# RG-LRU and multiplicative feed-forward on one core: the order of the jobs and the engines of some of them set anew

## The chip, the core and the metric

The kernel runs on one core of a Trainium2 chip, in one launch. The metric is the device time of that launch in microseconds (us): the median of three runs before the change is 511.52 us (511.37, 511.52 and 512.6).

## The reference

A gated linear recurrence over time (RG-LRU) is followed by a multiplicative feed-forward network. Four sequences of 5824 steps and 256 channels come in as `x`, with a recurrence gate `r_gate` and an input gate `i_gate` of the same shape.

```python
log_a = 8.0 * sigmoid(r_gate) * log(sigmoid(a_param))
a_t   = exp(log_a)
x_g   = sqrt(max(1 - a_t * a_t, 1e-6)) * sigmoid(i_gate) * x
h     = a_t[:, t] * h + x_g[:, t]          # for each t, h = 0 at t = 0
y[:, t] = h
out   = (((y @ w1) * (y @ w2)) @ w3) @ w_out   # 256 -> 1024, 1024 -> 1024 -> 256
```

The kernel folds `w3 @ w_out` once into one matrix of 1024 x 256, so a token costs two products of 256 x 1024 and one of 1024 x 256.

## The kernel before

The 23296 tokens (batch and time in one row) are cut into 47 chunks: two of 256 tokens (chunks 0 and 1, whose gates are computed together as chunk 0), 44 of 512 and a last one of 256. Each chunk goes through a chain of small jobs. A job is written as a letter with the chunk's number, then the number of the half, the quarter or the bank:

- `r`, `i`, `x` load a chunk's gate and input rows (SyncE's DMA queue, SP in the profile), `o` stores output rows.
- `R`, `I` are the two tanh on ScalarE (ACT); a sigmoid is 0.5 (1 + tanh).
- `V` turns the recurrence gate so that channels lie on partitions: by TensorE (PE, line 200) for the chunks in `TURN_R`, by a transposing DMA for all others.
- `d` is the decay a_t on ACT (line 223), one job for each half of the channels, and `s` its square (lines 231 and 233).
- `q` is the square root on ACT (line 238), in place in the tile `nrm`.
- `p` (1 + tanh) runs on GpSimd (POOL); `t` multiplies it by x, into the tile `u_t` (lines 189 and 192). `U` turns u as `V` does the gate.
- `g` combines root and u on VectorE (DVE, lines 248 and 251). `h` is the scan over time, DVE's alone (line 270). `y` casts it to bfloat16 (lines 280 and 282).
- `a` and `b` are the two up-projections on PE (line 299). `a` fills one bank of 512 columns, which `c` copies to SBUF (tile `sa`, lines 320 on DVE and 322 on ACT). `b` fills two banks, which `m` multiplies by `sa` on DVE, into `g_t` (line 337).
- `D` is the down-projection on PE (line 357), `e` copies its output out of PSUM (tile `ot`).
- `Lw`, `Cw` load and cast weights; `Ft`, `Fc`, `Fm`, `Fe` fold w3 and w_out in eight pieces (line 425 transposes, line 436 multiplies into `pw`); `W` is a pair of warm matmuls whose result is not used (line 287).

So `a4.2.1` is the first up-projection of chunk 4, third quarter, second half of it, and `m4.2` the product of that quarter.

There are 2449 jobs. One string, `ORDER`, lists them all, and the loop below it calls each in turn, so an engine executes its jobs in the order in which the string names them. Nothing reorders them on the engine: a job that waits holds up what stands behind it on that engine. Sets of tuples say which engine does a job that several can do: `DV_COPY` for `c`, `DV_EVAC` for `e`, `DV_SQUARE` and `AC_SQUARE` for `s` (POOL otherwise), `DV_HALF` for `t`, `DV_CAST` and `AC_CAST` for `y` (POOL otherwise), `FOLD_ACT` for `Fc` and `Fe` (DVE otherwise).

Buffers are rings (`RINGS`), taken in the order of the string. PSUM has four banks in the ring `po`, which `a`, `V`, `U`, `Ft`, `Fm` and `D` share, and two pairs of banks in the ring `pb` for `b` and `W`. A matmul that takes a bank waits until the one four back (two back for `b`) has been read.

Of the kernel before, what the change touches and what calls it, by code (L numbers as in the profile page):

```python
# [23 lines left out]
def kernel(  # L24
# [150 lines left out]
    def times(c, half):  # L175
# [15 lines left out]
        else:  # L191
            (nc.vector if (c, half) in DV_HALF else nc.gpsimd).tensor_mul(out=u, in0=t, in1=xt)  # L192

# [31 lines left out]
    def square(c, cb):  # L225
# [6 lines left out]
        else:  # L232
            (nc.vector if (c, cb) in DV_SQUARE else nc.gpsimd).tensor_mul(out=n, in0=a, in1=a)  # L233

# [37 lines left out]
    def cast(c, cb=None):  # L272
# [8 lines left out]
        else:  # L281
            (nc.vector if key in DV_CAST else nc.gpsimd).tensor_copy(out=y, in_=h)  # L282

# [190 lines left out]
    def last(c):  # L474
# [26 lines left out]
        Lw3.4 x3 Lw3.3 Lw3.6 Lw3.7 r7 m0.2 h2.0 h2.1 R3 a1.2.1 a1.2.0 a0.3.0 c1.3.0 c0.3.0 Fm2 b0.3 b1.2 V3 R4 V4
        c1.2.0 d3.1 d4.0 d3.0 d4.1 m0.3 b1.3 y2 Fe2 m1.2 m1.3 a2.0.0 a2.0.1 b2.0 a2.1.0 c2.0.1 c2.0.0 c2.1.0 m2.0
        Cw3.0 s3.1 Cw3.5 Cw3.1 b2.1 a2.2.1 Ft0 a2.1.1 Fc0 Ft1 c2.1.1 Fc1 s4.0 I3 s4.1 c2.2.1 a2.2.0 Ft5 Fm0 p3 Cw3.4
        c2.2.0 Fc5 m2.1 s3.0 q3 Cw3.3 Fe0 b2.3 Fm1 q4 Fe1 Ft4 t3.0 t3.1 U3 Fc4 g3 h3.0 h3.1 Cw3.6 Cw3.7 b2.2 Fm5 Fm4
        a2.3.1 Ft7 R7 Fe5 Fe4 Fc7 r5 i4 r6 x4 i5 i6 i7 c2.3.1 a2.3.0 Ft3 R5 I4 c2.3.0 Fc3 Ft6 Fm7 y3 a3.2.1 Fc6 Fm3
        m2.3 R6 Fe7 c3.2.1 V7 m2.2 Fe3 d7.1 a3.2.0 c3.2.0 d7.0 b3.2 Fm6 a3.3.1 a3.0.0 a3.3.0 m3.2 Fe6 c3.0.0 I5 c3.3.1
        s7.0 I6 V5 r8 i8 V6 r9 x5 b3.3 d5.1 a3.0.1 d5.0 c3.0.1 c3.3.0 m3.3 p4 t4.0 t4.1 p5 s7.1 U4 a3.1.1 c3.1.1 s5.0
        I7 I8 D0.1 D0.0 b3.0 b3.1 a3.1.0 g4 h4.0 h4.1 s5.1 R8 R9 d6.0 d6.1 p6 y4 p8 t5.0 t5.1 D0.3 D0.2 m3.0 e0.0
        c3.1.0 a4.1.1 b4.1 a4.3.1 D2.0 D2.1 s6.1 q7 e2.0 q5 s6.0 x6 p7 t6.0 t6.1 c4.1.1 e0.1 m3.1 c4.3.1 x7 x8 o0.0
        i10 r11 V9 o2.0 a4.0.1 a4.1.0 c4.0.1 c4.1.0 m4.1 a4.2.0 b4.3 a4.3.0 U5 g5 h5.0 h5.1 c4.2.0 c4.3.0 q6 D2.3 D2.2  # L510
        e2.1 r12 r10 V8 o2.1 o0.1 i9 i11 x10 a4.0.0 U6 D3.0 a4.2.1 D3.1 b4.0 c4.0.0 I10 c4.2.1 e3.0 d9.1 d9.0 m4.3 g6
        y5 t8.1 t7.1 t7.0 m4.0 a5.1.0 b4.2 a5.1.1 a5.0.1 a5.0.0 b5.0 c5.1.1 c5.1.0 c5.0.0 m4.2 h6.1 U7 a5.3.1 c5.0.1
        s9.1 R10 c5.3.1 R11 d8.1 I9 m5.0 g7 h6.0 b5.1 D3.3 b5.3 D3.2 a5.2.1 a5.3.0 e3.1 R12 d8.0 m5.1 c5.2.1 c5.3.0
        h7.1 D4.2 a5.2.0 D4.3 e4.1 m5.3 i13 V10 o3.0 x9 p10 t8.0 y6 p9 s8.0 s9.0 h7.0 b6.0 a6.0.0 a6.0.1 y7 c5.2.0 I11
        I13 a6.2.1 a6.2.0 b5.2 s8.1 c6.0.0 c6.0.1 c6.2.0 D4.1 a6.1.0 D4.0 d10.1 c6.2.1 d10.0 e4.0 q9 a6.1.1 m6.0 m5.2
        U8 o3.1 i12 r15 V11 r13 t9.1 t9.0 U9 V12 a6.3.0 b6.1 c6.1.1 c6.1.0 m6.1 a6.3.1 b6.2 a7.1.1 b6.3 a7.1.0 m6.2
        t10.0 s10.1 p11 t10.1 o4.0 o4.1 r16 i14 i16 c6.3.0 q8 c6.3.1 m6.3 g8 h8.0 h8.1 g9 c7.1.1 c7.1.0 a7.3.0 a7.0.0
        a7.0.1 b7.1 c7.3.0 R15 c7.0.0 c7.0.1 D6.0 D6.1 a7.3.1 D5.0 D6.2 b7.3 D6.3 D5.1 d11.1 c7.3.1 e6.0 s11.1 I12
        d11.0 d12.1 m7.1 h9.1 y8 a7.2.1 a8.2.0 b7.0 e6.1 m7.3 p12 s11.0 p13 s10.0 e5.0 a8.2.1 a7.2.0 c7.2.1 I16 c8.2.1
        s12.1 m7.0 c8.2.0 a8.0.1 b7.2 c8.0.1 c7.2.0 a8.0.0 c8.0.0 m7.2 D5.2 D5.3 b8.0 a8.1.1 d12.0 R13 q10 q11 c8.1.1  # L520
        I14 x11 o6.0 t11.0 t11.1 U10 r14 x12 o6.1 x13 V13 b8.2 D7.1 D7.0 h9.0 m8.0 g10 e5.1 y9 t12.1 V15 U11 o5.0 o5.1
        m8.2 b8.1 a8.1.0 c8.1.0 a9.1.0 a9.0.1 h10.0 h10.1 m8.1 e7.0 R16 c9.1.0 c9.0.1 d13.1 a9.0.0 b9.0 c9.0.0 D7.2
        a8.3.1 a9.1.1 D7.3 c9.1.1 R14 d15.0 e7.1 c8.3.1 y10 p16 a8.3.0 b9.1 d13.0 o7.0 x15 x14 i15 V14 o7.1 r17 t13.0
        p14 s13.1 t12.0 t13.1 m9.0 m9.1 a10.0.0 b8.3 d15.1 c8.3.0 c10.0.0 s12.0 s15.1 a9.2.1 a10.3.1 a10.0.1 b10.0
        a9.2.0 c9.2.1 m8.3 g11 c10.3.1 c10.0.1 m10.0 c9.2.0 d14.0 b9.2 D8.1 a10.3.0 a9.3.1 D8.0 h11.0 c10.3.0 e8.0
        d14.1 I15 D8.2 D8.3 e8.1 V16 d16.0 s13.0 a9.3.0 b10.3 d16.1 c9.3.1 h11.1 m9.2 U12 U13 r19 o8.0 r20 i17 x16 i19
        a10.2.0 a10.2.1 b9.3 a10.1.1 c10.2.1 c10.2.0 R17 m10.3 c9.3.0 m9.3 b10.2 c10.1.1 s14.0 y11 p15 t14.0 s16.1
        t15.1 t15.0 s16.0 t14.1 a10.1.0 a11.0.1 c10.1.0 m10.2 c11.0.1 a11.1.0 a11.3.0 b10.1 a11.0.0 a11.1.1 c11.1.0
        m10.1 q12 s14.1 c11.3.0 c11.0.0 q13 a11.2.0 b11.0 c11.1.1 g12 m11.0 b11.1 D10.3 a11.3.1 D10.2 s15.0 q14
        c11.2.0 c11.3.1 e10.1 a11.2.1 b11.3 D10.0 q15 D10.1 e10.0 c11.2.1 q16 D9.1 h12.0 h12.1 g13 y12 m11.1 h13.1  # L530
        h13.0 a12.0.1 b11.2 D9.2 a12.0.0 D9.0 D9.3 c12.0.1 R19 c12.0.0 U15 x17 U14 o8.1 o10.1 V17 d17.0 I17 r18 r23
        y13 V19 m11.3 m11.2 e9.0 e9.1 b12.0 m12.0 a13.0.0 a12.2.0 c12.2.0 b12.1 a12.1.0 t16.0 t16.1 U16 o10.0 o9.0 g14
        h14.0 h14.1 a12.1.1 c13.0.0 R18 c12.1.0 g15 a13.0.1 d17.1 V18 a12.2.1 b12.2 d19.0 D11.0 R20 c12.1.1 c12.2.1
        c13.0.1 r21 p17 y14 s19.0 D11.1 D11.2 a12.3.0 D11.3 m12.1 b13.0 e11.0 d19.1 e11.1 m12.2 d18.0 a12.3.1 a14.0.0
        s18.0 m13.0 c12.3.0 I19 c12.3.1 a13.1.0 b12.3 i20 V20 x19 b14.0 a14.0.1 c14.0.0 h15.0 d18.1 a13.1.1 m12.3
        c14.0.1 a13.2.0 s17.0 t17.0 c13.1.0 c13.2.0 m14.0 c13.1.1 b13.1 a14.1.0 m13.1 R21 a14.1.1 a13.2.1 i18 c14.1.0
        I20 c13.2.1 c14.1.1 r22 o9.1 V21 t17.1 o11.0 h15.1 a13.3.0 b14.1 g16 m14.1 i21 o11.1 c13.3.0 D12.0 D12.1 h16.0
        I18 a13.3.1 a14.2.1 b13.2 a14.2.0 m13.2 c13.3.1 e12.0 o12.0 d20.0 d20.1 p19 R22 c14.2.0 D12.2 b13.3 D12.3
        c14.2.1 y15 s18.1 b14.2 a15.0.0 a15.0.1 e12.1 m13.3 c15.0.0 c15.0.1 s19.1 m14.2 a15.1.0 a14.3.0 a15.1.1 h16.1
        p20 s20.0 c15.1.0 c15.1.1 b15.0 c14.3.0 m15.0 b15.1 a14.3.1 a15.2.0 x20 a15.2.1 x18 D13.0 r25 U17 R23 x21  # L540
# [124 lines left out]
```

## Time and profile before

| what | us |
|---|---|
| median of three runs | 511.52 |
| lowest and highest | 511.37, 512.6 |
| span of the profiled execution | 509.1 |
| median less that span | 2.4 |

The profiled execution is one run of the program on the chip, and its span runs from its first to its last instruction; of its time only this span is shown. A row of the timeline has the start, the duration, the engine, the line, the operation, output and inputs with their shapes, how many instructions are merged in it, and, in brackets, how long the engine had been idle and what released it. A group's row has the busy time of all its instructions, the mean duration of one in ns, and the idle time before them. PEld is the loading of weights into the array, which goes on beside the matmuls.

### The profile page before, as it was taken

Reading aid. Unit: us, or ns where it says so; the run is one execution under the profiler, and the core shown is the slowest. Engines: PE = TensorE matmul, PEld = TensorE weight load, DVE = VectorE, ACT = ScalarE, POOL = GpSimd, SP = SyncE. Lnnn points to the kernel's source line nnn. Section 1 sums busy time; section 2 is a strip of 40 time slices with the busy share of each in tenths; the row PEclk is TensorE's granted clock in tenths of the full one; section 3 lists DMA queues with packets and bytes.
Section 4 is the critical chain, followed back from the end, with each engine's and each line's share of the span. In section 5 each row is a group of like instructions: output and inputs, shape, how many; then the busy total and the mean of one; then the engine's idle time right before and its main releaser. Section 6 shows DMA issues by size and latency. Waiting matters only on the chain.

```text
span 509.1 us, 8891 instructions
## 1 busy us (share of the span) xinstructions
PE 501.7 (99%) x3225; PEld 308.3 (61%) x3225; DVE 431.8 (85%) x417; ACT 461.5 (91%) x708; POOL 318.0 (62%) x269
## 2 busy tenths in 40 slices
...
GB/s 317 410 411 345 335 316 282 305 286 259 310 220 298 279 285 247 211 302 196 247 305 327 254 286 148 252 243 227 210 246 164 235 298 161 85 166 62 65 51 104
DMA packets 178048, 124.06 MB, mean 244 GB/s; under 512 B 87378, under 2 KB 174036, under 8 KB 178004
## 3 DMA queue, kind: packets, MB, share of 16 engines
...
## 4 chain that ended last, share of the span: by engine, by line
PE 92%; ACT 3%; DMA 2%; POOL 1%; DVE 1%; issue 1%; SPq 1%; ACTq 0%; DVEq 0%
PE po L357 30%; PE pb L299 29%; PE pa L299 29%; DMA wf<-in_moe_w_dram 2%; PE pw L436 1%; ACT sa L322 1%; PE ptr L200 1%; PE ptw L425 1%; POOL u_t L192 0%; DVE h_t L270 0%; SPq L151 0%; ACT ot L322 0%; SPq L407 0%; ACT L168 0%; ACT L238 0%
## 5 line engine op out<-in xcount | busy, mean ns | idle before, releaser
L337 DVE TENSOR_TENSOR g_t<-sa,pb 128x1024 bf16<-128x1024 bf16 (+1 forms) x188 | 218.7, 1180 | 58.9 <-PE pb L299 27.6
L299 PEld LDWEIGHTS <-w_sb 128*128 128x128 bf16 x1504 | 146.4, 98 | 144.1 <-issue 1.4
L322 ACT CAST sa<-pa 128x512 bf16<-128x512 f32 (+1 forms) x332 | 179.8, 591 | 27.1 <-PE pa L299 18.9
L299 PE MATMUL pa<-y_t,w_sb 128*128 128x512 bf16 (+1 forms) x752 | 190.2, 372 | 0.2 <-ACT sa L322 0.2
L299 PE MATMUL pb<-y_t,w_sb 128*128 128x512 bf16 (+1 forms) x752 | 184.9, 372 | 0.2 <-ACT w_sb L414 0.2
L357 PE MATMUL po<-wp_sb,g_t 128*128 128x256 bf16 (+1 forms) x1464 | 177.6, 272 | 0.0
L357 PEld LDWEIGHTS <-g_t 128*128 128x128 bf16 x1464 | 142.5, 98 | 39.5 <-issue 0.3
L282 POOL CAST y_t<-h_t 128x1024 bf16<-128x1024 f32 (+2 forms) x47 | 53.8, 1145 | 140.2 <-DVE h_t L270 136.1
L192 POOL TENSOR_TENSOR u_t<-i_t,x_t 128x512 bf16<-128x512 f32 (+1 forms) x90 | 123.3, 1387 | 3.8 <-DMA ut<-u_t 1.8
L270 DVE TENSOR_TENSOR_SCAN h_t<-a_t,h_t,nrm 128x512 f32<-128x512 f32 (+1 forms) x92 | 121.1, 1343 | 1.6
L233 POOL TENSOR_TENSOR nrm<-a_t 128x512 f32<-128x512 f32 x70 | 78.4, 1137 | 7.0 <-ACT a_t L223 4.0
L223 ACT ACTIVATE a_t<-rt,la 128x512 f32<-128x512 bf16 (+1 forms) x82 | 66.1, 823 | 0.0
L322 ACT COPY ot<-po 128x512 f32<-128x512 f32 x84 | 49.1, 589 | 13.2 <-PE po L357 12.9
L173 POOL TENSOR_SCALAR i_t<-i_t 128x1024 f32<-128x1024 f32 (+1 forms) x45 | 55.4, 1233 | 8.3 <-ACT i_t L168 8.3
L251 DVE SCALAR_TENSOR_TENSOR nrm<-nrm,ut 128x1024 f32<-128x1024 f32 (+1 forms) x39 | 53.2, 1365 | 5.2 <-ACT nrm L238 5.2
L168 ACT ACTIVATE i_t<-i_t 128x1024 f32<-128x1024 f32 (+1 forms) x46 | 48.5, 1063 | 0.3 <-DMA i_t<-in_i_gate_dram 0.2
L238 ACT ACTIVATE nrm<-nrm 128x1024 f32<-128x1024 f32 (+1 forms) x47 | 48.4, 1040 | 0.2
L162 ACT ACTIVATE th_r<-r_t 128x1024 bf16<-128x1024 f32 (+1 forms) x41 | 43.5, 1064 | 0.0
L320 DVE CAST sa<-pa 128x512 bf16<-128x512 f32 x36 | 23.5, 684 | 1.4 <-PE pa L299 0.8
L238 ACT ACT_TABLE_LOAD x17 | 21.8, 1283 | 0.4
L287 PE MATMUL warm<-ident 128*128 128x512 bf16 x32 | 10.7, 473 | 1.6 <-DVE ident L441 1.6
L231 ACT ACTIVATE nrm<-a_t 128x512 f32<-128x512 f32 x18 | 11.4, 645 | 0.0
...
## 6 DMA issues: line engine op xcount, KB each, us to landing
...
wf<-in_moe_w_out_dram SPq DMA_DIRECT2D x2, 512.0 KB, 10.2
rt<-th_r SPq DMA_TRANSPOSE x41, 4.7
ut<-u_t SPq DMA_TRANSPOSE x39, 4.4
```

The lines of the kernel that those rows point to most:

```text
L173: (nc.vector if c in DV_PLUS else nc.gpsimd).tensor_scalar(t, t, 1.0, 1.0, op0=ALU.add, op1=ALU.mult)
L192: (nc.vector if (c, half) in DV_HALF else nc.gpsimd).tensor_mul(out=u, in0=t, in1=xt)
L223: nc.scalar.activation(out=a, in_=pr, func=AF.Exp, scale=la4[:, cb:cb + 1], bias=la4[:, cb:cb + 1])
L233: (nc.vector if (c, cb) in DV_SQUARE else nc.gpsimd).tensor_mul(out=n, in0=a, in1=a)
L238: nc.scalar.activation(out=n, in_=n, func=AF.Sqrt, scale=-1.0, bias=1.0)
L251: nc.vector.scalar_tensor_tensor(out=n, in0=n, scalar=1e-3, in1=T["pu", c][:, :, cols], op0=ALU.max, op1=ALU.mult)
L270: nc.vector.tensor_tensor_scan(h[:, cb, :], a[:, cb, :], n[:, cb, :], init, ALU.mult, ALU.add)
L282: (nc.vector if key in DV_CAST else nc.gpsimd).tensor_copy(out=y, in_=h)
L299: nc.tensor.matmul(out=dst, lhsT=w_sb[:, cb, m * P:(m + 1) * P], rhs=T["y", gates_of(c)][:, cb, span(c, mp)], start=(cb == 0), stop=(cb == ...
L322: nc.scalar.copy(out=dst, in_=src_ps)
L337: nc.vector.tensor_mul(out=T["g", z][:, 2 * mp:2 * mp + 2, span(c, mp)], in0=T["sa", c, mp][:, :, :w], in1=T["pb", c, mp][:, :, :w])
L357: nc.tensor.matmul(out=po, lhsT=T["g", c][:, k, j * P:(j + 1) * P], rhs=wp_sb[:, k, cols], start=(k == 0), stop=(k == KD - 1), skip_group_ ...
```

## The change

The string `ORDER` is new up to the jobs of chunk 24, and the same, job for job, behind that. The sets of engines are new up to chunk 28. No job is added, dropped or computed in another way; tiles, rings and DMA sizes are the same. A part of the diff, the sets:

```diff
-    DV_HALF = set()
-    DV_SQUARE = {(0, 0), (0, 1), (5, 1), (9, 0)}
...
-    DV_CAST = {(1, 1)}
-    AC_CAST = {(1, 0)}
+    DV_HALF = {(5, 0), (17, 0)}
+    DV_SQUARE = {(0, 0), (0, 1), (3, 1), (13, 0), (18, 1), (19, 1), (21, 0), (23, 1), (24, 1), (28, 0)}
...
+    DV_CAST = {24, (0, 1), (1, 1)}
+    AC_CAST = {14}
...
-    DV_EVAC = {(0, 0), (0, 1), (4, 1), (5, 1), (6, 1), (9, 0), (9, 1)}
-    FOLD_ACT = {('e', 0), ('e', 4), ('e', 5), ('e', 7)}
+    DV_EVAC = {(0, 0), (0, 1), (4, 0), (5, 1), (6, 1), (9, 0), (9, 1), (12, 1), (13, 0), (20, 0), (22, 1)}
+    FOLD_ACT = {('e', 0), ('e', 3), ('e', 4), ('e', 5), ('e', 6), ('e', 7)}
...
-        r0 i0 x0 Lw1.1 Lw1.0 r2 i2 Lw2.0 Lw3.2 x2 E W13 A3. A0. A1. A2. R0.1 R0.0 W3 W10 V0.0 V0.1 I0 t0.1 d0.0 s0.0
+        r0 E W7 W1 A3. A0. i0 W8 A1. A2. R0.1 W14 R0.0 I0 V0.1 V0.0 x0 t0.0 W0 Lw1.1 W5 d0.0 s0.0 t0.1 U0 d0.1
```

Job by job, 34 go from ACT to DVE, 11 from POOL to DVE, 14 from DVE to ACT, 6 from ACT to POOL, 4 from POOL to ACT and 1 from DVE to POOL. DVE's balance is a gain of 30 jobs, nearly all of them in chunks 13 to 24.

PE's list in the start: the 16 pairs of warm matmuls are spread in another way. Before, three pairs stand ahead of V0 (the turn of chunk 0's gate), three between V0 and U0, seven between U0 and the first up-projection, and three among the up-projections of chunks 0 and 1. Now it is four, two, nine and one; that last one (W3) stands right behind Fm2, the first fold.

DVE in the first 15 us, before: from the first half of u of chunk 0 to the first copy of an up-projection.

```order
L189 SCALAR_TENSOR_TENSOR u_t<-i_t,x_t 128x512
L233 TENSOR_TENSOR nrm<-a_t 128x512 x2
L189 SCALAR_TENSOR_TENSOR u_t<-i_t,x_t 128x512
L416 CAST w_sb<-wf 128x2x512
L248 SCALAR_TENSOR_TENSOR nrm<-nrm,ptr 128x256 x2
L270 SCALAR_TENSOR_TENSOR h_t<-a_t,nrm 128x256 x2
L248 SCALAR_TENSOR_TENSOR nrm<-nrm,ptr 128x256 x2
L270 SCALAR_TENSOR_TENSOR h_t<-a_t,h_t,nrm 128x256 x2
L282 CAST y_t<-h_t 128x256
L320 CAST sa<-pa 128x2x256 x2
```

The same place now (the code's lines lie two further down).

```order
L191 SCALAR_TENSOR_TENSOR u_t<-i_t,x_t 128x512
L235 TENSOR_TENSOR nrm<-a_t 128x512
L191 SCALAR_TENSOR_TENSOR u_t<-i_t,x_t 128x512
L235 TENSOR_TENSOR nrm<-a_t 128x512
L418 CAST w_sb<-wf 128x2x512
L250 SCALAR_TENSOR_TENSOR nrm<-nrm,ptr 128x256 x4
L272 SCALAR_TENSOR_TENSOR h_t<-a_t,nrm 128x256 x2
L284 CAST y_t<-h_t 128x256
L272 SCALAR_TENSOR_TENSOR h_t<-a_t,h_t,nrm 128x256 x2
L322 CAST sa<-pa 128x2x256
L284 CAST y_t<-h_t 128x256
L322 CAST sa<-pa 128x2x256
```

The second half of u has moved between the squares, the combine of chunk 1 ahead of the scans of chunk 0, and a cast of y has come to DVE.

POOL in the first 26 us, before: from the cast of w1 to the cast of chunk 2's y.

```order
L416 CAST w_sb<-wf 128x2x512
L282 CAST y_t<-h_t 128x256 x2
L416 CAST w_t<-wf 128x1024
L173 TENSOR_SCALAR i_t<-i_t 128x1024
L192 TENSOR_TENSOR u_t<-i_t,x_t 128x512 x2
L416 CAST w_sb<-wf 128x2x512
L416 CAST wo_sb<-wf 128x1024 x2
L282 CAST y_t<-h_t 128x1024
```

And now.

```order
L418 CAST w_sb<-wf 128x2x512
L284 CAST y_t<-h_t 128x256
L175 TENSOR_SCALAR i_t<-i_t 128x1024
L284 CAST y_t<-h_t 128x256
L418 CAST w_t<-wf 128x1024
L194 TENSOR_TENSOR u_t<-i_t,x_t 128x512 x2
L418 CAST w_sb<-wf 128x2x512
L418 CAST wo_sb<-wf 128x1024 x2
L284 CAST y_t<-h_t 128x1024
```

One of chunk 0's two casts of y has left POOL and one of chunk 1's has come, and `p` of chunk 2 (line 175) stands ahead of the cast of a piece of w3.

DVE around chunks 14 and 15, before: from the scan of chunk 15's second half to the combine of chunk 17.

```order
L270 SCALAR_TENSOR_TENSOR h_t<-a_t,h_t,nrm 128x512
L251 SCALAR_TENSOR_TENSOR nrm<-nrm,ut 128x1024
L337 TENSOR_TENSOR g_t<-sa,pb 128x1024
L270 SCALAR_TENSOR_TENSOR h_t<-a_t,h_t,nrm 128x512
L337 TENSOR_TENSOR g_t<-sa,pb 128x1024 x3
L270 SCALAR_TENSOR_TENSOR h_t<-a_t,h_t,nrm 128x512
L337 TENSOR_TENSOR g_t<-sa,pb 128x1024 x3
L251 SCALAR_TENSOR_TENSOR nrm<-nrm,ut 128x1024
```

And now, from the same scan to the second copy behind it of an up-projection.

```order
L272 SCALAR_TENSOR_TENSOR h_t<-a_t,h_t,nrm 128x512
L194 TENSOR_TENSOR u_t<-i_t,x_t 128x2x2x128
L322 CAST sa<-pa 128x512
L339 TENSOR_TENSOR g_t<-sa,pb 128x1024
L272 SCALAR_TENSOR_TENSOR h_t<-a_t,h_t,nrm 128x512
L339 TENSOR_TENSOR g_t<-sa,pb 128x1024
L322 COPY ot<-po 128x512
L339 TENSOR_TENSOR g_t<-sa,pb 128x1024
L235 TENSOR_TENSOR nrm<-a_t 128x512
L339 TENSOR_TENSOR g_t<-sa,pb 128x1024
L235 TENSOR_TENSOR nrm<-a_t 128x512
L322 CAST sa<-pa 128x512
```

Between products and scans stand a half u, copies out of PSUM (`sa`, `ot`) and squares that were ACT's or POOL's.

More of the change, by code (lines that the diff above doesn't have):

```diff
@@ L501 @@
[L501 to L540, printed above, removed]
@@ new lines @@
+        c6.1.0 R12 p11 d10.0 o3.1 q9 D4.0 e4.0 p10 x11 a6.1.1 b6.1 c6.1.1 a6.3.1 s10.1 m6.1 r14 b6.2 m6.2 a7.3.0
+        s8.1 a6.3.0 c6.3.0 a7.1.0 c7.3.0 q8 c6.3.1 b6.3 c7.1.0 m6.3 a7.3.1 I12 t9.1 p13 x10 t10.1 r15 g8 c7.3.1
+        t10.0 V11 U9 g9 d11.1 a7.0.1 c7.0.1 o4.0 h8.0 a7.1.1 h8.1 h9.1 c7.1.1 b7.1 m7.1 o4.1 x12 D6.1 D6.0 e6.0
+        i16 I16 r16 b7.3 d11.0 V12 U10 s11.1 d12.1 m7.3 a7.0.0 D5.0 c7.0.0 D5.1 e5.0 d12.0 D6.2 p16 a7.2.1
+        c7.2.1 D6.3 e6.1 b7.0 m7.0 x13 y8 a8.2.1 a8.2.0 s10.0 c8.2.0 a7.2.0 c7.2.0 a8.0.1 c8.0.1 c8.2.1 t11.1
@@ new lines @@
+        a8.0.0 c8.0.0 r13 R13 V13 o6.0 R15 V15 q10 b7.2 m7.2 h9.0 s11.0 q11 d13.0 o5.0 a8.1.1 c8.1.1 D5.3 D5.2
+        e5.1 t13.0 d15.1 D7.0 b8.0 m8.0 t11.0 y9 b8.2 R14 m8.2 p12 D7.1 e7.0 i15 g10 h10.0 h10.1 t13.1 a8.1.0
+        c8.1.0 b8.1 m8.1 a9.1.0 d13.1 a9.0.1 y10 b9.0 a9.0.0 c9.0.0 o6.1 i14 c9.1.0 D7.3 U11 c9.0.1 x15 t12.1
+        d15.0 D7.2 a8.3.1 c8.3.1 e7.1 a8.3.0 R16 r17 V14 d14.0 a9.1.1 m9.0 c9.1.1 i17 o5.1 b9.1 b8.3 a10.0.0
+        c10.0.0 r19 c8.3.0 m9.1 V16 a10.3.0 c10.3.0 x16 a10.3.1 c10.3.1 m8.3 o7.0 a10.0.1 c10.0.1 g11 d14.1
@@ new lines @@
+        t17.1 U17 e12.1 m13.3 o11.1 a15.1.1 s19.1 c15.1.1 a15.0.1 b14.2 m14.2 c15.0.1 a15.1.0 c15.1.0 R23
+        a14.3.0 s20.1 s18.1 c14.3.0 p18 b15.0 m15.0 V21 d21.0 a14.3.1 b15.1 t18.1 c14.3.1 a15.2.1 c15.2.1 h16.1
+        a15.2.0 D13.3 d21.1 c15.2.0 D13.1 x21 D13.0 e13.0 m15.1 s17.1 q17 x19 y16 b14.3 q18 a16.0.0 m14.3 D13.2
+        e13.1 c16.0.0 t19.0 b15.2 m15.2 t18.0 U18 x20 i22 a16.1.0 c16.1.0 q19 o12.1 a16.1.1 g17 x22 s20.0 t19.1
+        U19 V22 c16.1.1 a15.3.0 c15.3.0 a16.0.1 c16.0.1 b16.0 q20 m16.0 a16.2.0 h17.0 h17.1 c16.2.0 b15.3 t20.0
@@ new lines @@
+        s25.1 a19.2.1 c19.2.1 b19.2 x24 D17.1 c19.3.0 s23.1 b19.3 m19.2 s21.1 c19.3.1 m19.3 e17.0 o17.0 r28 q21
+        V26 g21 t23.0 a20.0.1 c20.0.1 a20.1.0 b20.0 a20.0.0 o16.0 c20.1.0 c20.0.0 a20.2.0 c20.2.0 a20.2.1
+        c20.2.1 x25 a20.1.1 c20.1.1 D17.2 t23.1 D17.3 b20.1 r29 p25 x27 a20.3.0 R30 V27 h21.0 h21.1 m20.0 e17.1
+        a20.3.1 I24 m20.1 y21 a21.0.0 U23 s24.1 q24 r34 t25.0 c20.3.1 b20.2 t25.1 c21.0.0 D18.1 c20.3.0 x26
+        b21.0 m20.2 a21.1.0 i27 D18.0 e18.0 g22 h22.0 q25 h22.1 y22 D18.2 D18.3 a21.0.1 e18.1 o18.1 c21.1.0
@@ new lines @@
+        b24.0 c24.0.0 c24.0.1 m24.0 h26.0 q28 D22.3 I32 y25 d32.0 D23.0 x30 b24.1 m24.1 D22.2 e22.1 e23.0 b24.2
+        I30 t28.1 V29 t28.0 h26.1 x29 a24.3.0 c24.3.0 g27 a24.3.1 a24.2.1 c24.3.1 b24.3 I29 c24.2.1 D23.2 r31
+        m24.2 m24.3 R31 D23.3 a25.0.0 i31 o21.1 a25.0.1 e23.1 c25.0.0 a25.1.1 a25.1.0 d32.1 c25.0.1 c25.1.0
+        c25.1.1 y26 a25.2.1 d29.0 x31 h27.0 r33 i34 b25.0 b25.1 s30.0 s30.1 s32.0 a25.2.0 c25.2.0 c25.2.1 m25.0
+        m25.1 a25.3.0 a25.3.1 b25.2 o22.1 U28 b25.3 x32 R34 p30 a26.0.0 c25.3.0 V31 o23.0 h27.1 d29.1 t30.0 p29
```

216 lines of the change are left out of this document (120 added, 96 removed), and 8 rows, old and new, of the table DV_COPY.

## The prediction

> **What bounds the kernel now.** I read the page first, then the groups of PE by shape, the chain that ended last, the table by stretches of 20 us, and last the first 36 us of the timeline. Page, then groups:
>
> ```profile
> span 509.1 us, 8891 instructions
> PE 501.7 (99%) x3225; PEld 308.3 (61%) x3225; DVE 431.8 (85%) x417; ACT 461.5 (91%) x708; POOL 318.0 (62%) x269
> ```
>
> ```profile
> L299 PE MATMUL pa<-y_t,w_sb 128*128 128x512 bf16 x704 | 183.0, 379 | 0.2 <-ACT sa L322 0.2
> L299 PE MATMUL pb<-y_t,w_sb 128*128 128x512 bf16 x704 | 178.0, 379 | 0.0
> L357 PE MATMUL po<-wp_sb,g_t 128*128 128x256 bf16 x1448 | 176.7, 273 | 0.0
> ```
>
> A matmul's own time (379 ns) overlaps its neighbours', so the pace is read where the chain that ended last has PE alone (start, us, what):
>
> ```profile
> 131.52 1.73 PE pb L299 x8
> 136.72 2.62 PE po L357 x24
> ...
> 502.45 3.53 PE po L357 x40
> ```
>
> That is 0.216 us for 512 columns and 0.109 for 256. 1408 x 0.216 + 1448 x 0.109 = 462 us. The rest after the start (weight folds, transposes, the short last chunk) I put at 16 us from the counts in the kernel at the same pace: 478. Chunk 2's first full-width matmul starts at 26.4 (row below) and the last matmul ends at 502.45 + 3.53 = 506.0, so in 479.6 us PE loses about 1.4. The last copy and store take the 3.1 us that remain. PE is a wall; an order can only move the time at which PE gets going, those 1.4 us, and waits that it adds.
>
> The other engines by stretch (PE, PEld, DVE, ACT, POOL busy; clock; DMA share; GB/s):
>
> ```profile
> 100.00:120.00 20.00, 20.00 (x121) 11.66 (x120) 19.90 (x22) 19.04 (x28) 14.70 (x12) 1.00 1.13 291
> 140.00:160.00 20.00, 20.00 (x122) 11.74 (x121) 19.25 (x19) 19.56 (x30) 13.23 (x11) 1.00 0.92 259
> 160.00:180.00 20.00, 20.00 (x126) 12.19 (x125) 15.95 (x13) 19.29 (x32) 17.58 (x15) 1.00 1.03 273
> 180.00:200.00 20.00, 20.00 (x126) 12.14 (x125) 18.01 (x15) 19.07 (x30) 10.94 (x9) 1.00 0.93 280
> 200.00:220.00 20.00, 20.00 (x119) 11.37 (x117) 16.95 (x14) 19.54 (x32) 17.36 (x15) 1.00 0.88 223
> 220.00:240.00 20.00, 20.00 (x124) 11.95 (x123) 17.16 (x15) 19.91 (x29) 10.70 (x10) 1.00 0.79 229
> 240.00:260.00 20.00, 20.00 (x131) 12.57 (x130) 16.93 (x15) 19.93 (x34) 15.73 (x13) 1.00 1.04 279
> 260.00:280.00 20.00, 20.00 (x132) 12.66 (x130) 17.71 (x15) 19.85 (x31) 13.19 (x11) 1.00 1.09 313
> ```
>
> PE is full in every one. Up to 160 DVE and ACT are full too (0.10 and 0.75 us of DVE idle in the first two rows) and still feed PE; after that DVE has slack and ACT has not.
>
> **The start, step by step.** Timeline of the first 36 us (start, duration, engine, line, what; idle before and releaser in brackets):
>
> ```profile
> 6.32 2.77 PE L287 MATMUL warm<-ident 128*128 128x512 bf16 x6
> 7.08 0.69 DVE L189 SCALAR_TENSOR_TENSOR u_t<-i_t,x_t 128x512 bf16<-128x512 f32 x1 [1.62 <-DMA x_t<-in_x_dram]
> 7.69 1.29 DVE L233 TENSOR_TENSOR nrm<-a_t 128x512 f32<-128x512 f32 x2
> 9.31 1.15 ACT L238 ACTIVATE nrm<-nrm 128x512 f32<-128x512 f32 x2
> ...
> 10.09 3.19 PE L287 MATMUL warm<-ident 128*128 128x512 bf16 x14
> 10.36 0.75 DVE L248 SCALAR_TENSOR_TENSOR nrm<-nrm,ptr 128x256 f32<-128x256 f32 x2 [0.18 <-PE ptr L200]
> 11.14 1.37 DVE L270 TENSOR_TENSOR_SCAN h_t<-a_t,nrm 128x256 f32<-128x256 f32 x2
> 11.99 1.06 POOL L282 CAST y_t<-h_t 128x256 bf16<-128x256 f32 x2 [0.61 <-DVE h_t L270]
> 13.11 1.04 PE L299 MATMUL pa<-y_t,w_sb 128*128 128x256 bf16 x8
> 13.19 1.39 DVE L270 TENSOR_TENSOR_SCAN h_t<-a_t,h_t,nrm 128x256 f32<-128x256 f32 x2
> 15.22 0.61 PE L299 MATMUL pb<-y_t,w_sb 128*128 128x256 bf16 x4 [0.19 <-ACT w_sb L414]
> 17.35 0.69 DVE L320 CAST sa<-pa 128x512 bf16<-128x512 f32 x1 [0.79 <-PE pa L299]
> 17.52 2.50 POOL L192 TENSOR_TENSOR u_t<-i_t,x_t 128x512 bf16<-128x512 f32 x2
> 19.15 0.68 DVE L320 CAST sa<-pa 128x512 bf16<-128x512 f32 x1
> 19.17 1.06 ACT L238 ACTIVATE nrm<-nrm 128x1024 f32<-128x1024 f32 x1
> 19.75 1.28 DVE L337 TENSOR_TENSOR g_t<-sa,pb 128x512 bf16<-128x512 bf16 x2
> 20.94 1.28 DVE L248 SCALAR_TENSOR_TENSOR nrm<-nrm,ptr 128x512 f32<-128x512 f32 x2
> 20.95 2.02 POOL L416 CAST wo_sb<-wf 128x1024 bf16<-128x1024 f32 x2
> 22.73 2.49 DVE L270 TENSOR_TENSOR_SCAN h_t<-a_t,h_t,nrm 128x512 f32<-128x512 f32 x2
> 23.04 1.04 PE L436 MATMUL pw<-wo_sb,w3t 128*128 128x256 bf16 x8
> 25.28 1.04 POOL L282 CAST y_t<-h_t 128x1024 bf16<-128x1024 f32 x1 [2.32 <-DVE h_t L270]
> 26.38 1.02 PE L299 MATMUL pa<-y_t,w_sb 128*128 128x512 bf16 x4
> ```
>
> Back to back, DVE's starts lie 0.60 us apart for 512 columns (19.15 to 19.75).
>
> *Later:* DVE now does u, square, u, square from 7.08, so the second square ends about 9.56, not 8.98; the root that follows started only at 9.31, 0.33 behind the square, so it moves by 0.3. The first combine starts near 10.25. Both combines (0.78 each) now stand ahead of chunk 0's scans: scans at 11.8 instead of 11.14, their end 13.15, POOL's cast of one half (0.53 of the pair's 1.06) and the hand-over: PE's first real matmul about 13.75, not 13.11. Cost 0.65 there. It lands on nothing at first: pb cannot start before its weight cast on ACT (15.22 before; ACT does the same list up to it).
>
> *Earlier:* one half of y has gone from POOL to DVE, and POOL takes the +1 of chunk 2 ahead of a weight cast that had waited for its DMA. POOL then reaches u of chunk 2 about 16.8 instead of 17.52 and ends the two wo casts about 22.3 instead of 22.97. On DVE the copy that idled 0.79 us for PE (17.35) now follows two products, and a transposition no longer stands ahead of its matmuls. From chunk 1's scans (end 14.56) DVE has two copies, half a y cast (0.18), two products, three copies, two products: 9 x 0.60 + 0.18 = 5.6, so 20.15. Chunk 2's combine then waits for its root (19.17 + 1.06 = 20.23): 20.3 against 20.94. Scans and cast follow: y of chunk 2 ends about 25.7 instead of 26.3.
>
> PE's list in that stretch has one pair of warm matmuls where before had three pairs behind the first real one; but PE must wait for wo at the fold (22.35, was about 23.2: the pair of rows at 23.04). Behind the fold it has before's list plus that one pair (0.43). So chunk 2 starts 0.85 - 0.43 = 0.4 us earlier. Bounds: 0.75 earlier if the fold waits less, 0.4 later if the array's clock is late (below). I take -0.4.
>
> **The middle.** Three terms.
> - *Old gaps.* About half of the 1.4 us I put where the order is changed (up to chunk 24, by its share of the time); it can vanish wholly or stay: -0.2 of 0 to -0.6. The other half is behind chunk 24, where the list of jobs is word for word the same.
> - *Up to chunk 6.* PE takes a2.1.1 as soon as V4's bank is read by both decays of chunk 4, which ACT finishes about when PE asks. And until m5.0 DVE has some 0.5 us more work (one more copy and one more half u at 0.60, two small weight folds less). ACT and DVE are full here, so I put 0.2 back, of 0 to 1.0.
> - *Chunks 13 to 24.* 29 steps of about 0.60 us move to DVE (17 copies, 4 evacuations, 6 squares, half a u, one y): 17.4 us. DVE's idle time in the six rows from 160 to 280 is 4.05 + 1.99 + 3.05 + 2.84 + 3.07 + 2.29 = 17.3. ACT is rid of 21 copies, which buys nothing, as ACT does not hold PE there. DVE becomes as full as it is at 100 to 120, where PE lost nothing. I take +0.3, of 0 to 2.5.
>
> The edits that leave DVE for ACT or POOL in chunks 5 to 12 I cost at nothing: POOL is idle a third of the time, and ACT's share of copies falls as much as its squares rise.
>
> Sum: -0.4 - 0.2 + 0.2 + 0.3 = -0.1. The profiled execution spans 509.1; the median of the three times is 511.52, so 2.4 us lie outside the span and stay. Forecast 511.4.
>
> **The rivals.**
>
> *DVE takes over (slower).* POOL and DVE get in each other's way: this combine waited out a POOL square.
>
> ```profile
> 192.98 1.03 POOL L233 TENSOR_TENSOR nrm<-a_t 128x512 f32<-128x512 f32 x1
> 193.20 1.90 DVE L251 SCALAR_TENSOR_TENSOR nrm<-nrm,ut 128x1024 f32<-128x1024 f32 x1
> ```
>
> It took 1.90 us and ended 1.09 us after the square. Before had idle time on DVE to absorb that. With none left, the waits that a full DVE still has (0.10 to 0.75 us per 20, say 0.4, over six stretches) reach PE: about 2.5 us instead of 0.3, so 513.6. It decides once DVE has less than some 0.4 us of slack per 20. For it: the two sums are equal. Against it: 40 to 160, just as full, where PE held, and POOL has fewer squares to collide with. 17%. [...]
>
> *All goes well (faster).* Chunk 2 starts 0.75 us earlier and the 1.4 us of gaps vanish: 511.5 - 2.15 = 509.4. It needs the unchanged tail to lose its gaps too. 10%.
>
> *The array's clock comes late (no change).* Six warm matmuls at 6.32 took 0.46 us each, fourteen at 10.09 took 0.23: the array reached its full pace in between. Now four stand before U0 instead of six, and eighteen behind. If those start slow, some seven of them cost 0.2 us more: the first real matmul comes 1.2 us later still, DVE's waits for it take up 0.4 of that, and chunk 2 starts 0.8 us later than forecast, 0.4 later than before: 512.2. 7%. [...]
>
> That the change does nothing at all is excluded: the instructions stand on other engines.
>
> **The numbers.** A measurement of this kernel tells about 0.3% (1.5 us) from no change: faster is under 510.0, slower over 513.05. Forecast as worked out 61%, clock 7%, both within; DVE 17%, and 5% for a late transfer, since SP's queue is reordered in full, both slower; faster 10%. So 0.10, 0.68, 0.22. The range takes in the faster rival's edge and the DVE rival: 509.7 to 513.8.
>
> **What would show it.** Right: first pa near 13.75, chunk 2's first matmul near 26.0, PE at 20.00 in every stretch, DVE over 19 in all stretches from 160 to 280, ACT under 19. Wrong: PE under 19.8 anywhere after 30, combines or scans over 1.8 us with PE waiting for products behind them (DVE rival); 512-column warm matmuls over 0.4 us after 10 (clock); a start of chunk 2 before 25.7 with a shorter tail (faster).

## The result and the profile after

The change made the kernel slower: 532.35 us (median of five runs, 531.28 to 533.73) against 511.49 us of the kernel before on the same chip (511.37 to 512.6). The ratio is 1.0409, with a 95% interval of 1.0392 to 1.0425: 20.9 us. The page of the changed kernel begins:

```profile
span 531.1 us, 8854 instructions
PE 503.2 (95%) x3169; PEld 308.1 (58%) x3225; DVE 450.4 (85%) x447; ACT 454.2 (86%) x686; POOL 304.9 (57%) x261
```

PE has 95% of a longer span, and no other engine has a larger share than before. (56 records of matmuls are missing here, 3169 against 3225, while the weight loads are complete. In the trace each leaves a hole of about 0.05 us that is no idle time, 3.0 us in all; a stretch with 19.8 to 19.9 of 20 us may be full.) PE's large groups by shape, with the idle time ahead of them and who ended it:

```profile
L301 PE MATMUL pa<-y_t,w_sb 128*128 128x512 bf16 x670 | 181.6, 381 | 13.2 <-ACT ot L324 6.2 <-ACT sa L324 4.8 <-POOL y_t L284 0.4
L359 PE MATMUL po<-wp_sb,g_t 128*128 128x256 bf16 x1448 | 177.0, 273 | 2.1 <-ACT sa L324 1.4
L301 PE MATMUL pb<-y_t,w_sb 128*128 128x512 bf16 x682 | 175.6, 380 | 4.7 <-DVE g_t L339 3.8
```

A matmul costs what it cost (381 ns against 379). Idle time is new: 13.2 us ahead of `pa` where there were 0.2, 4.7 and 2.1 ahead of `pb` and `po` where there were none, 20.0 us together, of which 3.0 are those holes. By stretches of 20 us (PE, PEld, DVE, ACT, POOL busy; clock; DMA share; GB/s):

```profile
20.00:40.00 20.00, 19.43 (x177) 14.16 (x180) 19.80 (x29) 19.55 (x28) 13.34 (x14) 1.00 1.04 410
40.00:60.00 20.00, 18.22 (x134) 12.21 (x135) 17.80 (x22) 18.69 (x26) 14.10 (x14) 1.00 1.07 308
...
100.00:120.00 20.00, 17.41 (x96) 9.72 (x97) 16.34 (x17) 19.08 (x28) 12.05 (x11) 0.91 0.92 216
...
200.00:220.00 20.00, 16.77 (x103) 10.03 (x103) 18.81 (x17) 12.83 (x22) 10.34 (x8) 1.00 0.96 259
```

PE is no longer full, and DVE and ACT have room where PE starves: at 100 to 120 DVE has 3.7 us to spare, at 200 to 220 ACT has 7. The engines wait for each other in a ring, and something else lets the first of them run late. The waits of all engines name it (us in total, times, longest):

```profile
POOL u_t L194 <- DMA x_t<-in_x_dram: 12.6, 9, 3.8
ACT a_t L225 <- DMA rt<-th_r: 8.6, 5, 2.6
ACT i_t L170 <- DMA i_t<-in_i_gate_dram: 7.3, 5, 3.6
PE pa L301 <- ACT ot L324: 6.2, 7, 1.5
ACT ot L324 <- DMA out_dram<-ot: 4.2, 5, 1.7
```

In the same view of the kernel before, POOL's u never waits for x_t, ACT never for rt nor for a store, and ACT waits 0.2 us for i_t in all. The first of PE's new gaps shows how it works. SyncE's queue around 40 us (start, us, what):

```profile
40.03 4.18 SPq L213 DMA_TRANSPOSE rt<-th_r  x2
44.26 0.57 SPq L153 DMA_DIRECT2D i_t<-in_i_gate_dram  x1
44.88 0.98 SPq L153 DMA_DIRECT2D r_t<-in_r_gate_dram  x2
45.90 0.51 SPq L153 DMA_DIRECT2D x_t<-in_x_dram  x1
```

A piece of the chain that ended last, and the rows of DVE and PE behind it (idle time and its releaser in brackets):

```profile
45.90 7.89 DMA x_t<-in_x_dram
```

```profile
53.89 0.89 DVE L194 TENSOR_TENSOR u_t<-i_t,x_t 128x512 bf16<-128x512 f32 x1 [1.75 <-DMA x_t<-in_x_dram]
54.71 1.21 DVE L339 TENSOR_TENSOR g_t<-sa,pb 128x1024 bf16<-128x1024 bf16 x1
...
55.97 1.02 PE L301 MATMUL pb<-y_t,w_sb 128*128 128x512 bf16 x4 [1.50 <-DVE g_t L339]
```

The load at 45.90 is x5, whose buffer had been free since u of chunk 0 was done, before 10 us. It is asked for behind V5 and V6, the two turns at 40.03, which wait for ACT's tanh; it takes 7.89 us; DVE, which now makes half of chunk 5's u, waits 1.75 us for it, its next product stands behind that, and PE stands still for 1.50 us. The kernel before asks for x5 even later, at 47.3, but its job t5.0 stands so much later that it starts at 54.9 without a wait. A load is late only in relation to the place of its reader.

Counted over all loads of x issued between 40 and 300 us, from the issue on SP to the start of the first reader: the median was 16.6 us before and is 10.6 now, and 11 of 27 have less than 8 us, where 3 of 29 had. For the turns V: 9.5 and 7.0, and 16 of 26 under 8 us, where 8 of 28 were. From issue to landing such a transfer takes 5.4 us in the median, and over 8.3 for the slowest in twenty. The count is a hint and no measure of the loss, as two of the experiments below show.

### The profile page after: what moved, and what is told of

Read it like the earlier page. It is cut to its first block, busy times and chain, and to the rows that moved or that the text cites. A ratio compares the mean times of both kernels' runs of the same rounds, so it can differ in the third digit from the quotient of the medians.

```text
span 531.1 us, 8854 instructions
## 1 busy us (share of the span) xinstructions
PE 503.2 (95%) x3169; PEld 308.1 (58%) x3225; DVE 450.4 (85%) x447; ACT 454.2 (86%) x686; POOL 304.9 (57%) x261
## 4 chain that ended last, share of the span: by engine, by line
PE 54%; DMA 15%; ACT 14%; issue 6%; DVE 5%; SPq 4%; POOL 1%; ACTq 0%; DVEq 0%; POOLq 0%
PE pb L301 17%; PE pa L301 17%; PE po L359 17%; ACT sa L324 5%; DMA out_dram<-ot 4%; DMA rt<-th_r 4%; DMA wf<-in_moe_w_dram 4%; DVE g_t L339 3%; DMA x_t<-in_x_dram 2%; SPq L213 2%; ACT ot L324 2%; ACT a_t L225 2%; SPq L153 2%; ACT th_r L164 2%; DVE h_t L272 1%
## 5 line engine op out<-in xcount | busy, mean ns | idle before, releaser
L324 ACT CAST sa<-pa 128x512 bf16<-128x512 f32 (+1 forms) x314 | 170.1, 588 | 34.8 <-PE pa L301 24.1
L301 PE MATMUL pb<-y_t,w_sb 128*128 128x512 bf16 (+1 forms) x730 | 182.3, 373 | 5.4 <-DVE g_t L339 3.8
L194 POOL TENSOR_TENSOR u_t<-i_t,x_t 128x512 bf16<-128x512 f32 (+1 forms) x88 | 122.7, 1408 | 18.6 <-DMA x_t<-in_x_dram 12.6
L284 POOL CAST y_t<-h_t 128x1024 bf16<-128x1024 f32 (+2 forms) x45 | 47.0, 1045 | 141.6 <-DVE h_t L272 141.6
L272 DVE TENSOR_TENSOR_SCAN h_t<-a_t,h_t,nrm 128x512 f32<-128x512 f32 (+1 forms) x92 | 117.7, 1309 | 1.7 <-DVE nrm L253 0.5
L235 POOL TENSOR_TENSOR nrm<-a_t 128x512 f32<-128x512 f32 x66 | 74.1, 1137 | 14.2 <-ACT a_t L225 10.3
L175 POOL TENSOR_SCALAR i_t<-i_t 128x1024 f32<-128x1024 f32 (+1 forms) x45 | 53.6, 1193 | 21.8 <-ACT i_t L170 14.2
L253 DVE SCALAR_TENSOR_TENSOR nrm<-nrm,ut 128x1024 f32<-128x1024 f32 (+1 forms) x39 | 55.7, 1431 | 6.3 <-ACT nrm L240 4.0
L324 ACT COPY ot<-po 128x512 f32<-128x512 f32 x80 | 46.6, 585 | 16.8 <-PE po L359 11.5
L322 DVE CAST sa<-pa 128x512 bf16<-128x512 f32 x54 | 36.0, 682 | 2.6 <-remote 1.1
L322 DVE COPY ot<-po 128x512 f32<-128x512 f32 (+2 forms) x13 | 8.1, 633 | 4.2 <-PE po L359 3.5
```

The costliest lines, as they stand in the source:

```text
L175: (nc.vector if c in DV_PLUS else nc.gpsimd).tensor_scalar(t, t, 1.0, 1.0, op0=ALU.add, op1=ALU.mult)
L253: nc.vector.scalar_tensor_tensor(out=n, in0=n, scalar=1e-3, in1=T["pu", c][:, :, cols], op0=ALU.max, op1=ALU.mult)
L272: nc.vector.tensor_tensor_scan(h[:, cb, :], a[:, cb, :], n[:, cb, :], init, ALU.mult, ALU.add)
L301: nc.tensor.matmul(out=dst, lhsT=w_sb[:, cb, m * P:(m + 1) * P], rhs=T["y", gates_of(c)][:, cb, span(c, mp)], start=(cb == 0), stop=(cb == ...
L324: nc.scalar.copy(out=dst, in_=src_ps)
```

## The experiments

My theory after the traces (S): the new order of SyncE's list asks for transfers too late for the new places of their readers. Rivals: the DMA engines are simply too full (D), the new lists of the compute engines hold PE up by themselves (K), the new sets of engines do (E). Each ratio is against the kernel before, run beside it, and the last column is worked out from the ratio.

| kernel | median us | ratio, 95% interval | over the kernel before, us |
|---|---|---|---|
| the changed kernel | 532.35 | 1.0409 (1.0392 to 1.0425) | 20.9 |
| SP's list alone reordered | 518.18 | 1.0127 (1.0112 to 1.0142) | 6.5 |
| eleven jobs of SP's list moved | 520.73 | 1.0187 (1.0164 to 1.0211) | 9.6 |
| of these, the seven loads | 525.98 | 1.0289 (1.0272 to 1.0307) | 14.8 |
| of these, three turns and a store | 530.62 | 1.0368 (1.0334 to 1.0402) | 18.8 |
| changed kernel, loads halved | 512.55 | 1.0021 (1.0012 to 1.0031) | 1.1 |
| kernel before, loads halved | 511.57 | 0.9997 (0.9988 to 1.0007) | -0.2 |
| kernel before, two SP jobs later | 525.58 | 1.0272 (1.0258 to 1.0287) | 13.9 |
| old order, new engine sets | 535.63 | 1.0468 (1.0453 to 1.0483) | 23.9 |
| the same, loads halved | 536.14 | 1.0476 (1.0461 to 1.0492) | 24.3 |
| new order, old engine sets | 555.49 | 1.0870 (1.0846 to 1.0894) | 44.5 |
| changed kernel, x loaded by POOL's queue | 562.93 | 1.1001 (1.0965 to 1.1037) | 51.2 |
| new start, old rest | 511.91 | 1.0011 (1.0001 to 1.0020) | 0.6 |

**SP's list alone.** The lists of PE, ACT, DVE and POOL are the changed kernel's, row for row. SP's jobs from x4 on, the beginning of the new list:

```diff
-x4 i5 V5 V6 i7 r9 r8 x5 i8 x6 r11 V9 o0.1 o0.0 V8 x7 o2.0 x8 i10 r12 r10 o3.0 i9 x9 i11
+x4 i5 x5 V5 V6 i7 r9 r8 i8 x6 r11 V9 o0.1 o0.0 V8 x7 o2.0 x9 i10 r10 i9 i11 x8 i13 o2.1
...
```

> The new kernel with only SyncE's list changed: loads, transposing DMAs and stores stand in another order on SP (over 40 of them moved forward past others, each with the jobs that it feeds in mind); the lists of PE, ACT, DVE and POOL and all engine sets are those of the new kernel, instruction for instruction. Theory S (the new order of SP's list asks for transfers behind others that are still waiting, so they land after their readers are ready): half to three quarters of the 20.8 us come back, 516 to 522 us, and the long waits on x_t, i_t and rt shrink. Rival D (the DMA engines are simply full, transfers would be late in any order): 530 to 534 us. Rival K (the new lists of ACT, DVE and POOL hold PE up whatever the transfers do): 528 to 534 us.

Measured 518.18 us, 14.4 of the 20.9 us back, with the same bytes on the same DMA engines and nothing else touched. D and K fall as sole causes. The wait for x_t falls from 12.6 to 9.1 us, those for rt, i_t and stores from 8.6, 7.3 and 4.2 to 0.3, 1.1 and 0.3. What the 6.5 us that remain are was not taken apart by itself; the largest wait for a transfer that is left behind the start is that for x_t.

**Eleven moves.** Two places of SP's list:

```diff
-x4 i5 V5 V6 i7 r9 r8 x5 i8 x6 r11
+x4 i5 x5 V5 V6 i7 r9 r8 i8 x6 r11
...
-r16 V12 U10 x13 r13 V13 o6.0 V15 o5.0 i15 o6.1 i14 U11
+r16 V12 U10 r13 x13 i15 o6.0 V13 V15 o5.0 o6.1 i14
...
```

> As the run before, but only eleven of SyncE's 324 jobs are moved forward in the new kernel: x5 ahead of V5, x10 by 13 places, V22 by 6, i15 by 4, U15 and U27 by 3, i32 by 2, and r13, x20, r25 and o6.0 by 1. Theory S: each of the places is one of the gaps of PE, worth about 1 to 2 us with what follows; some 8 to 13 us of 20.8 come back, 519 to 525 us. PE's gap of 1.67 us at 54 us goes, since x5 is asked for about 5 us sooner. Rivals D and K: 530 to 534 us.

Measured 520.73 us: 11.3 us hang on the places of eleven DMA issues among 324. DVE's half of chunk 5's u, in this kernel's timeline:

```profile
52.16 0.67 DVE L194 TENSOR_TENSOR u_t<-i_t,x_t 128x512 bf16<-128x512 f32 x1
```

It starts 1.73 us sooner and waits for nothing (no bracket), and PE's gap there is gone.

**The eleven in two parts.** In the first, x5, x10, i15, i32, r13, x20 and r25 move and the others stay; in the second, V22, U15, U27 and o6.0 move.

> Of the eleven moves in SyncE's list that gave back 11.6 us, only the seven loads: x5, x10, i15, i32, r13, x20 and r25 ahead. Theory S with separate prices (each late transfer costs its own gap of PE, and what follows keeps the distance): about 6 to 8 us back, 524 to 526.5 us, and this run's gain and that of the other four moves add up to 11.6 us within 2 us. Rival C (a chain: a later transfer is late because of the earlier one, so that one part undoes all or nothing): 521 us or 531 us.

> Of the same eleven moves only the turns V22, U15 and U27 and the store o6.0, which moves the loads named in the run beside it back. Theory S with separate prices: about 5 to 6 us back, 526 to 528 us; with the run beside it 11.6 us within 2 us. Rival C: 521 us or 531 us.

Measured: the loads give back 6.1 us, the other four 2.1, whose interval (17.1 to 20.6 us over) overlaps that of the changed kernel (20.1 to 21.7), so that they may give nothing alone. The first is as I expected, the second is not: 530.62 us, and not 526 to 528. Together they give 8.2 us, where both at once give 11.3 (I had expected 11.6 within 2): prices do not add up. It is no all-or-nothing chain either, since the loads alone give about half. Why they don't add up stays open.

**Loads of half the size.**

```diff
...
+        n = n // 2 if taken[nm] > RINGS[nm] else n
-        nc.sync.dma_start(out=T[nm, c][:, :n, cols], in_=rows[:, :, cols])
+        nc.sync.dma_start(out=T[nm, c][:, :n, cols], in_=rows[:, :n, cols])
...
```

> The new kernel, with every load of r, i and x behind the first one into each buffer bringing only half the rows (the other half of the buffer keeps what stood there, so the outputs are not the reference's); all instructions on the other engines are the same. Each load then moves 256 KB instead of 512 KB. Theories S and D (the lateness of transfers is what costs): landings come 1 to 3 us sooner each, 514 to 522 us. Theory K: 528 to 533 us.

> The kernel before, with the same halved loads. In its trace PE has no gap for a load, and the chain of waits that ended last is 2% DMA, so theories S, D and K all expect no change here, 510 to 512 us. If it falls as much as the halved loads of the new kernel do, halving helps for another reason than late transfers, and that run says nothing.

Measured 512.55 and 511.57 us. The old kernel does not care; the changed one gets back 19.8 of its 20.9 us, without one job moved, and more than the 514 to 522 us that I expected. Nor do the compute engines run faster with less traffic: a product takes 1211 ns (1212 with whole loads), ACT's copy of `sa` 594 (594), POOL's half of u 1406 (1424). Its stretches, of which two:

```profile
100.00:120.00 20.00, 19.89 (x120) 11.81 (x121) 19.65 (x21) 19.80 (x29) 11.25 (x10) 1.00 0.92 228
200.00:220.00 20.00, 19.89 (x112) 11.02 (x113) 18.14 (x18) 19.63 (x30) 14.82 (x13) 1.00 0.60 153
```

PE is full or nearly so on the same lists and sets, with the DMA share at 0.60 instead of 0.96 in the second stretch but at 0.92 as before in the first (0.73 instead of 0.95 in the mean from 40 to 300 us). So the share of one stretch does not tell; the time of a transfer has changed: the medians from issue to landing of r, i and x are 3.9, 3.4 and 3.4 us, where they were 6.0, 5.5 and 5.3. K can claim 1.1 us at most once transfers are quick. Order and load belong together: the new order of SP's list would do if transfers were quick, and the transfers would do in another order.

**The converse in the old kernel.** Every other engine's list is the old one.

```diff
-o10.1 V17 r18 r23 V19 U16
+o10.1 r18 r23 V19 V17 U16
...
-r30 o14.1 V24 x23 V27 U21 x24
+r30 V24 x23 V27 U21 o14.1 x24
```

> The kernel before with two of SyncE's 324 jobs moved back in its list and nothing else: V17 (a transposing DMA) by 3 places, behind r18, r23 and V19, and o14.1 (a store) by 4 places, behind V24, x23, V27 and U21. Theory S: a job that SP issues behind others that still wait holds up its reader, and the buffers behind it, and PE: from walking the lists with the mean durations of the trace, an estimate of 515 to 530 us. Rivals K and E (lists and sets of the compute engines): 511 to 512 us, since all those are as before.

Measured 525.58 us: two places cost 13.9 us. Its SP queue around V17, and then its waits:

```profile
138.56 1.09 SPq L151 DMA_DIRECT2D r_t<-in_r_gate_dram  x2
144.16 2.59 SPq L211 DMA_TRANSPOSE rt<-th_r  x2
```

```profile
ACT ot L322 <- DMA out_dram<-ot: 5.8, 1, 5.8
PE pa L299 <- ACT ot L322: 5.8, 1, 5.8
ACT a_t L223 <- DMA rt<-th_r: 5.0, 2, 3.7
```

V19 waits at the head of the list for its tanh until 144.14, and V17, whose own tanh was done at 128.9, cannot pass it and is issued at 145.4. ACT waits 3.7 us for it, PE 2.72. The store o14.1 was ready at 201.9 and is issued at 219.7, behind V27, which waited for its buffer: ACT has no free `ot`, PE no free bank, 5.8 us. PE is idle for 9.3 us in this trace; the half clock at both of these gaps (last section) comes on top.

**Sets and order apart.** Two kernels take one half of the change each.

> The kernel before, its order of jobs unchanged, with the new sets of engines alone. Theory S (the loss is in the order of SyncE's list) gives the sets no loss of their own: 511 to 514 us. Rival E (the new engine sets load DVE and ACT wrongly) puts at least half of the 20.8 us here: 522 us or more. A middle value would say that sets and order belong together: a job that goes to another engine stands in that engine's list at a place that was chosen for the old one.

> The new order of jobs, with the old sets of engines. Rival E: the loss goes with the sets, 511 to 520 us. Theory S: SyncE's list stays the new one, so the loss stays, 530 us or more; above 535 us if the new order relies on the new sets.

Measured 535.63 and 555.49 us: each half alone is worse than both together. My expectation for the first, that the sets have no loss of their own in the old order, was wrong. I then took it for the same cause, which the halved loads could test:

> The old order with the new sets of engines (535.6 us in an earlier run), and with the halved loads (the outputs are not the reference's). Theory S, widened after that run: what the sets change is when each buffer comes free and when each stored or turned tile is ready, so they set when SP's list can go on, and the loss is paid through late transfers again; with loads of half the time it nearly goes, 511 to 516 us. Rival E (the sets load ACT, DVE and POOL wrongly, whatever the transfers do): 528 us or more.

Measured 536.14 us: no gain at all. Theory S, widened in this way, falls for that kernel. Nor is it a blocked list of SP's, which lighter loads would not free: behind the first 15 us no engine waits for x, i, rt or a store in this trace, once 0.6 us for r and once 0.7 for ut. The longest of its PE waits are for DVE:

```profile
PE pb L307 <- DVE g_t L345: 6.8, 7, 2.8
PE po L365 <- DVE sa L328: 4.9, 1, 4.9
```

So sets that were chosen for one order hold up another by the compute engines' own lists. That is a second mechanism, and not that of the changed kernel, where the same sets lose 1.1 us at most once its loads are light.

**x by another queue.**

```diff
-        nc.sync.dma_start(out=T[nm, c][:, :n, cols], in_=rows[:, :, cols])
+        q = nc.gpsimd if nm == "x" and c >= 5 else nc.sync
+        q.dma_start(out=T[nm, c][:, :n, cols], in_=rows[:, :, cols])
...
```

> The new kernel with the loads of x from chunk 5 on issued by POOL's queue instead of SP's, each right behind the product t that frees its buffer, which POOL executes itself; all else in its order. No such load then stands behind a turn or a store that waits. Theory S (it is the place in SP's list): the 12.6 us that POOL waits for x_t fall to under 5 us, and a part of the loss comes back, 518 to 529 us; not all, since the waits for i_t, rt and ot remain, and x's transfers now run ahead of others on the same DMA engines. Rival D (the DMA engines are full, whoever asks): 530 to 534 us. If an issue costs POOL much time of its own, over 535 us with POOL's u_t late, and the run says nothing on S or D.

Measured 562.93 us, over the 535 from which, by my own words, the run says nothing on S or D. Its waits on DMA:

```profile
POOL u_t L195 <- DMA ut<-u_t: 27.3, 8, 9.8
ACT a_t L226 <- DMA rt<-th_r: 15.1, 8, 3.3
ACT ot L325 <- DMA out_dram<-ot: 10.9, 5, 7.7
...
POOL u_t L195 <- DMA x_t<-in_x_dram: 0.7, 2, 0.4
```

The wait for x falls from 12.6 to 0.7 us as expected, and the turns and stores pay: 27.3 for ut instead of 4.3, 15.1 for rt instead of 8.6, 10.9 for stores instead of 4.2. An issue also costs POOL itself 0.78 us, 32.8 us in all, so the run does not settle how much was crowding of the DMA engines and how much POOL's own time. By POOL's queue a load of x took 6.9 us from issue to landing, where it took 5.3 by SP's, and loads of i and the turns of u rose from 5.5 and 5.0 to 6.9 and 6.3 (loads of r fell from 6.0 to 5.6), so another queue made no room.

**The start alone.** The changed kernel's first 145 jobs, the old order and engines behind them.

> The new kernel's first 145 jobs, in its order and on its engines, up to the first up-projection of chunk 2; behind them all other jobs in the old order on the old engines. In the profile of the new kernel chunk 2's first matmul starts at 25.6 us, in that of the old one at 26.4 us. If the start keeps that gain and the rest stays full as before, 510.6 to 511.0 us, less than both kernels; if the loads and casts of the start that stand in other places make the old middle late, 512 to 514 us. Theory S has the loss behind 50 us, so nothing near 530 us.

Measured 511.91 us, no gain over the kernel before. In its trace chunk 2's first matmul starts at 26.14 us, and PE idles 0.89 us ahead of 31.97 and 0.26 ahead of 40.25, at the seam, which takes more than the start gained. I found no version that beats the kernel before; it fills PE from 26 us on. Deeper rings of buffers, which would let loads be asked for earlier, were not tried.

## Why the prediction was wrong, point by point

*PE as a wall.* Right: the pace is the same, and most of the loss is idle time of PE, 17.2 us in the trace without the holes. The rest is the clock (1.7 us, last section) and, by an estimate, 0.16 us at each of 24 gaps, 3.9 us, where a matmul's 0.379 us overlaps nothing ahead of it. Less the 0.7 us that the start gains, that makes 22.1; the two spans, 531.1 and 509.1, differ by 22.0. The sentence that an order can only move the start, the old gaps "and waits that it adds" held; I then priced the added waits for ACT and DVE alone.

*The start.* The sign was right, and the size about so. The rows of the changed kernel:

```profile
10.01 1.41 DVE L250 SCALAR_TENSOR_TENSOR nrm<-nrm,ptr 128x256 f32<-128x256 f32 x4
11.34 1.27 DVE L272 TENSOR_TENSOR_SCAN h_t<-a_t,nrm 128x256 f32<-128x256 f32 x2
13.13 1.03 PE L301 MATMUL pa<-y_t,w_sb 128*128 128x256 bf16 x8
25.64 1.03 PE L301 MATMUL pa<-y_t,w_sb 128*128 128x512 bf16 x3
```

The combines began at 10.01 and not 10.25, the scans at 11.34 and not 11.8; the first real matmul came at 13.13, not 13.75, so the 0.65 us that I put there did not come (four combines took 1.41 us, where I took 1.56), and chunk 2's first at 25.64, 0.74 earlier than before where I took 0.4. The bound of 0.75 held. But this is one execution: in the traces of the five kernels above that have the same start, SP's list reordered whole or in parts and loads halved, chunk 2 begins at 25.89 to 26.05, and in two more traces of the old start (loads halved, two jobs later) at 26.57 and 27.13. At 50 us the changed kernel was still about 0.4 us ahead, counted by PE's work so far.

*Up to chunk 6, and the old gaps.* The 1.4 us that I took PE to lose behind the start were not there. My own sum gives 479.6 - 478 = 1.6, and in the old trace PE is idle for 0.18 us between 26.4 us and its last matmul; the rest is the error of the 16 us that I put for folds and turns. So the -0.2 had nothing to come from, and "all goes well", which needed all 1.4, could not come true in full. For ACT and DVE being full I put 0.2 us; the first loss, 1.5 us at 54 to 56 us, came in this part from x5. Of t5.0, the half of u that went to DVE, I costed 0.60 us of DVE's time, and not that it had moved nearer to its load.

*Chunks 13 to 24.* The sum of 17.4 us to DVE was about right (450.4 against 431.8 us in all), but DVE was not what PE waited for: with the same sets and halved loads 1.1 us are left of 20.9.

*The step that failed* is the one that gave SyncE's queue no sum: "5% for a late transfer, since SP's queue is reordered in full". It named the cause, gave it 5%, and put no time on it: of the waits that the new order adds only those for DVE and ACT were summed. In its place the runs show SyncE's list as the price: in another order that list alone gives back 14.4 of the 20.9 us, and lighter loads in the same list 19.8. SP's list kept the relative order of 227 of 324 jobs, and my table showed the DMA share at 0.79 to 1.13 in each of its stretches. Both together make the loss: transfers that take 5 to 8 us, and a list that no longer fits its readers. What was missing was a walk through the lists that sets, for each load and turn, the place of its issue and what waits ahead of it against the place of its reader; such a walk gave 515 to 530 us for the old kernel with two jobs later. The bare count of short distances would not have done. With SP's list reordered, 8 of 27 loads of x and 19 of 28 turns have less than 8 us, and 6.5 us are lost; in the old kernel with two jobs later it is 1 of 28 and 8 of 27, and 13.9 are lost.

*The rivals.* "DVE takes over" had the right side and the wrong mechanism and size (513.6); a combine took 1.20 to 1.23 us in the old trace where POOL was idle beside it, against the 1.90 us of the row at 193.20. "All goes well" got its early start and lost it again. The array's clock came early, not late: it was full from 5.1 us on, and from 9.3 in the old trace (in the old kernel with two jobs later, whose start is the old one, the 32 warm matmuls took 9.4 us, 425 ns in the mean, where they took 10.7 and 473 in the old trace, so it differed between the two). That some seven matmuls behind U0 start slow no run shows: in the changed kernel the eighteen at 9.11 us took 4.05 us, 0.225 each. The clock did cost some 1.7 us in the middle (below). The range ended 18.5 us too low.
